# Three weight blocks of a folded product: turned by DMA in place of TensorE

## The chip, the cores and the metric

The kernel runs on one core of one Trainium2 chip. The metric is the device time of one execution in microseconds; the time before is the median of three runs. A profile shows one further execution, instruction by instruction. TensorE (PE) multiplies matrices, VectorE (DVE) and ScalarE (ACT) work on elements, GpSimd (POOL) does little here, and SyncE (SP) issues most DMAs.

## The reference

Attention without softmax is computed for 8 batches of 8 heads (576 tokens, 64 columns each), normalised, and fed as x (4608 x 512) to a multiplicative network:

```python
kv = np.einsum('bhsd,bhse->bhde', k, v)
out = np.einsum('bhsd,bhde->bhse', q, kv)
rms = np.sqrt(np.mean(out * out, axis=-1, keepdims=True) + 1e-06)
x = (out / rms * g_norm)        # then (B,H,S,D) -> (B*S, H*D)
a = x @ w1                      # 512 x 1024
b = x @ w2                      # 512 x 1024
h = a * b @ w3                  # 1024 x 1024
out = h @ w_out                 # 1024 x 512
```

The weights arrive as 64-bit floats, and the kernel makes 32-bit floats of them by itself.

## The kernel before, in words

There is no nonlinearity between w3 and w_out. The kernel therefore starts with a **fold**: it computes the product w3 @ w_out (1024 x 512) once and keeps it in `w3o_sb`. All the rest, for groups of 512 tokens, works with `w1`, `w2` and that product, by a fast matrix multiplication with seven products (lines L727, L1019, L1277).

The fold has two halves: half 0 takes the upper 512 rows of w3, half 1 the lower 512. Each half runs over eight chunks `c` of 128 columns of w3 and 128 rows of w_out (`KF` = 8). For a chunk, `fold_chunk` (L696) adds four products of 128x512 into four PSUM banks, one for each 128 rows `m`. TensorE needs its left operand transposed, so `turn_w3` (L683) first turns the four 128x128 blocks of a chunk by TensorE into a PSUM bank, and ScalarE copies that bank (L688) to the chunk's place in the tile `ab`. There are four such places, so chunks 4 and 5 write where chunks 0 and 1 stood. The profile records each 128x512 product as two matmul rows, and a chunk's four transposes as four.

Data come in this way. `load_next` issues on SP's queue the next load of a raw 64-bit tile `raw` (four buffers; a tile comes as a pair of DMAs). The conversion of a tile is ScalarE's L161 and L163, then VectorE's L165, L169, L172 and L175 (and L135 where a scale is applied). `begin_next` writes ScalarE's part, `end_next` writes VectorE's part and then the next load. For half 1 a raw tile holds two chunks of w3: chunks 2 and 3 are converted in step c = 0 of the second loop, chunks 4 and 5 in step c = 2, chunks 6 and 7 in step c = 4. Tiles of w1 and w2 are converted in the steps between.

Into the eight steps of half 1 the attention of batch 0 is woven: `begin_q` transposes q by TensorE (L358, copied by ScalarE, L360), `begin_kv` computes kv (L338, copied by L346 and L348), `product` multiplies them (L416). Its normalisation is ScalarE's L383 (squares), VectorE's L384, ScalarE's L388 (root), VectorE's L390 and L393, which write `xn`. Then `x_first` turns half of `xn` by DMA: ScalarE splits it into low and high 16-bit words (L297), SP issues two 16-bit DMA transposes (L301), and ScalarE joins the words (L311). The other half is transposed by TensorE (L452). These transposes and products, and those of chunks, share three PSUM banks (`ps_at`) in rotation; the sums of the fold lie in others.

What sets the order: in this part of the program all engines' instructions stand in the order in which the program writes them (`tc.manual_schedule` over the engines). An engine takes its own instructions strictly in that order and waits on semaphores for the others; SP's queue of DMA issues is such an order too. Behind the fold the order of VectorE and ScalarE is set by a scheduler.

Of the kernel before, what the change touches and what calls it, by code (L numbers as in the profile page):

```python
# [22 lines left out]
def kernel(  # L23
# [32 lines left out]
    nc = tc.nc  # L56
    PSUM = bass.MemoryType.PSUM
    P = 128
# [5 lines left out]
    KF = DF // P  # L64
# [19 lines left out]
    def bank(pool, tag):  # L84
        return pool.tile([P, 512], FP32, name=tag, tag=tag)
# [6 lines left out]
    def load_q(b, r):  # L92
        t = loaded["q", b, r] = inp.tile([P, 2, J * D], FP32, name="q_sb")
        nc.sync.dma_start(
            out=t, in_=q[b, 2 * r:2 * r + 2, 0:G, :].rearrange("h (p j) d -> p h (j d)", j=J)
        )
# [20 lines left out]
    ab = [ab_all[:, i] for i in range(2)]  # L117
# [71 lines left out]
    raws = []  # L189

    def raw_tile():
        return conv_pool.tile([P, 1024], w1.dtype, name="raw", bufs=RAW)

    def load_next():
        if len(raws) == len(todo):
            return
        what, i = todo[len(raws)]
        raw = raw_tile()

        def load(where, src):  # L200
            nc.sync.dma_start(out=raw[:, where].rearrange("p (c m) -> p c m", c=src.shape[1]), in_=src)

        if what == "w":
            for n, w in enumerate((w1, w2)):
                src = w[:, i * P:(i + 1) * P].rearrange("(c p) f -> p c f", p=P)
                load(slice(n * 512, (n + 1) * 512), src)
        elif what == "b":
            for h in range(2):
                src = w3[DF // 2:DF, (2 * i + h) * P:(2 * i + h + 1) * P]
                load(slice(h * 512, (h + 1) * 512), src.rearrange("(m p) f -> p m f", p=P))  # L210
        else:
            src = w3[0:DF // 2, i * P:(i + 1) * P].rearrange("(m p) f -> p m f", p=P)
            cols = w_out[i * P:(i + 1) * P, :].rearrange("p (c f) -> p c f", c=1)

            n = 1 if i else 2
            for h in range(n):
                load(slice(h * 512 // n, (h + 1) * 512 // n), src[:, h * NH // n:(h + 1) * NH // n, :])
            for h in range(n):
                f = slice(h * DM // n, (h + 1) * DM // n)
                load(slice(512 + f.start, 512 + f.stop), cols[:, :, f])  # L220
        raws.append(raw)
# [28 lines left out]
    def end_next(load=True):  # L250
        for c in begun[len(converted)]:
            all_of(c)
        converted.append(len(converted))
        if load:
            load_next()

    def all_of(steps):
        for _ in steps:
            pass
# [14 lines left out]
    def keep_warm(n):  # L274

        t = bank(ps_mm, "mm")
        for _ in range(n):
            nc.tensor.matmul(t[:, 0:P], lhsT=ident, rhs=ident, start=True, stop=True)

    def turn_by_dma(srcs, apart, turned, dsts, copy=nc.gpsimd.tensor_copy):  # L280

        def words(t):
            return t.bitcast(U16).rearrange("p ... (n w) -> p ... n w", w=2)

        def planes(t, i, n):
            t = t.bitcast(U16).rearrange("p (w n) -> p w n", w=2)
            size = 4 * P // n  # L290
            return t[:, :, i * size:(i + 1) * size]

        for i, src in enumerate(srcs):
            to = planes(apart, i, len(srcs))
            if len(src.shape) == 3:
                src, to = words(src), to.rearrange("p w (a n) -> p w a n", a=src.shape[1])
                copy(to, src.rearrange("p a n w -> p w a n"))  # L297
            else:
                copy(to, words(src).rearrange("p n w -> p w n"))
        yield  # L300
        nc.sync.dma_start_transpose(  # L301
            out=turned.bitcast(U16).rearrange("p (a t) -> p a t", t=P), in_=apart.bitcast(U16)
        )
        yield
        for i, dst in enumerate(dsts):
            src = planes(turned, i, len(dsts))
            if len(dst.shape) == 3:
                src = src.rearrange("p w (a n) -> p a n w", a=dst.shape[1])
            else:
                src = src.rearrange("p w n -> p n w")  # L310
            copy(words(dst), src)  # L311
# [364 lines left out]

    w3T = {}

    def turn_w3(half, c):
        t_ps = bank(ps_at, "at").rearrange("p (m f) -> p m f", m=NH)  # L680
        for m in range(NH):
            src = chunks[:, c, 0, m * P:(m + 1) * P]
            nc.tensor.transpose(t_ps[:, m, :], src, ident)  # L683

        w3T[half, c] = ab[c % 4 // 2][:, c % 2].rearrange(
            "p i (a f) -> p (i a) f", f=P
        )
        nc.scalar.copy(w3T[half, c], t_ps)  # L688

    sums_ps = {}  # L690

# [701 lines left out]
    chunks = fold.tile([P, KF, 2, DM], FP32, name="chunks")  # L1393
    with tc.manual_schedule(
        engines={mybir.EngineType.DVE, mybir.EngineType.Activation, mybir.EngineType.SP}
    ):
        for _ in range(RAW):
            load_next()
        nc.scalar.activation(const.tile([P, 1], FP32, name="warm"), eps_col, AF.Sqrt)
        g_row = const.tile([1, P], FP32, name="g_row")  # L1400
        for e in range(2):
            nc.scalar.dma_start(
                out=g_row[:, e * D:(e + 1) * D], in_=g_norm.rearrange("(o d) -> o d", o=1)
            )


        keep_warm(14)
        begin_next()
        end_next()
        turn_w3(0, 0)  # L1410
        keep_warm(6)
        begin_next()

        g_ps = bank(ps_at, "at")[:, 0:1]
        nc.tensor.transpose(g_ps, g_row, ident[0:1, 0:1])
        nc.scalar.copy(g_col, g_ps)
        for c in range(KF):

            if c > 2:
                begin_next()  # L1420
            end_next()
            if c == 4:
                load_four("k", 0, 0)
                load_q(0, 0)
            elif c == 5:
                load_four("v", 0, 0)
                load_q(0, 1)
                load_q_left(0)
            if c == 0:
                for n in range(2):  # L1430
                    fold_chunk(0, c, range(NH), slice(n * N, (n + 1) * N))
                begin_next(lambda: turn_w3(0, 1))
                keep_warm(2)
                continue
            fold_chunk(0, c, range(NH - 1))
            if c < 3:
                begin_next(lambda: turn_w3(0, c + 1), 2)
            else:
                turn_w3(*((0, c + 1) if c + 1 < KF else (1, 0)))
            fold_chunk(0, c, [NH - 1])  # L1440


        first = batch(0)
        first.start()
        BEGIN, PRODUCT = {1: 0, 4: 1}, {2: 0, 5: 1}
        norms = {}
        FIRST = len(converted) + KF - 1
        for c in range(KF):
            if c in BEGIN:
                first.begin_q(2 * BEGIN[c], 2 * BEGIN[c] + 1)  # L1450
                if c == max(BEGIN):
                    x_first = first.x_by_dma(0, nc.scalar.copy)
                    next(x_first)
                    next(x_first)
            if c - 1 in norms:
                all_of(norms[c - 1])
            if c < KF - 2:
                if c < max(BEGIN):
                    begin_next()
                if c == max(BEGIN) + 1:  # L1460
                    all_of(x_first)

                end_next(len(raws) < FIRST)
            elif c == KF - 2:
                run(sum_w(0))
            fold_chunk(1, c, [0])
            if c in BEGIN:
                first.begin_kv(BEGIN[c])
                if c == max(BEGIN):
                    load_q_left(1)  # L1470
            if c + 1 == KF:
                for r in range(2):
                    first.turn(2 + r)
                run(combine_x(0))
                end_next(False)
                for _ in range(3):
                    load_next()
            fold_chunk(1, c, range(1, NH - 1))
            if c + 1 < KF:
                turn_w3(1, c + 1)  # L1480
            if c in (max(BEGIN), KF - 2):
                begin_next()
            fold_chunk(1, c, [NH - 1])
            if c in PRODUCT:
                norms[c] = first.product(PRODUCT[c])
                next(norms[c])
                next(norms[c])
    fold_cm.__exit__(None, None, None)
    late_pool = ctx.enter_context(tc.tile_pool(name="late", bufs=1, reuse_waits="tile"))
# [6 lines left out]
    for n, T in enumerate(groups):  # L1496
# [29 lines left out]
        if T in IN_TWO:  # L1526
            p = 2
# [130 lines left out]
```

## Time and profile before

| | before |
|---|---|
| median of 3 runs | 742.34 us (741.92 to 742.8) |
| the profiled execution's own time | 742.22 us |
| its span, first to last instruction | 740.4 us |
| TensorE busy | 734.6 us |
| VectorE busy | 623.3 us |
| ScalarE busy | 379.4 us |
| mean granted TensorE clock | 1.000 |
| half 1 of the fold on TensorE | about 42 to 81 us |

Times in the profile are microseconds from the start of the span. A row of the order of time has the start, the length, the engine, the line of the program and the operation, the tiles (written <- read), and in brackets the engine's idle time ahead of it with what ended it. Such a length includes the time in which an instruction drains while the next begins, so the distance from one start to the next is what an instruction costs. A DMA has the time of its issue and, apart from it, the time from issue to landing.

### The profile page before, as it was taken

What the parts mean: (1) busy time and instruction counts of PE and PEld (TensorE: products, weight loads), DVE (VectorE), ACT (ScalarE), POOL (GpSimd) and SP (SyncE); (2) the same over time, 40 slices, a digit from 0 to 9 for tenths busy, and PEclk for the clock granted to TensorE, in tenths of its full rate; (3) what the DMA queues carried; (4) which work ended last, traced back from release to release, by engine and by line L of the source; (5) the groups of instructions that cost most, each with busy time, mean ns of one, the idle gap of its engine ahead of it and who ended that gap; (6) DMA issues with size and microseconds to landing.
All of it is one profiled execution on the core that took longest, in us unless ns stands there. A gap on an engine that the chain in (4) does not pass through costs nothing.

```text
span 740.4 us, 16858 instructions
## 1 busy us (share of the span) xinstructions
PE 734.6 (99%) x6845; PEld 659.8 (89%) x6845; DVE 623.3 (84%) x1253; ACT 379.4 (51%) x662; POOL 21.6 (3%) x29
## 2 busy tenths in 40 slices
PE   8999999999999999999999999999999999999998
PEld 6455788888899999999999999999999999999997
DVE  7967898967869689968996899689969987997797
ACT  6787777515552675257526752576177313212321
POOL 0000000131000000000000001000001000000000
PEclk9999999999999999999999999999999999999999
DMA  9997834599999698869886988688846762565454
GB/s 312 338 357 228 237 108 137 136 333 305 314 267 323 175 279 261 267 166 293 251 266 161 302 251 266 175 288 234 269 103 220 227 207 87 184 214 158 135 199 136
DMA packets 135457, 169.66 MB, mean 229 GB/s; under 512 B 78036, under 2 KB 110804, under 8 KB 135380
## 3 DMA queue, kind: packets, MB, share of 16 engines
q1 hardware_dynamic: 132928, 154.16, 69.1%
q10 hardware_dynamic: 2452, 14.42, 5.7%
q8 instruction: 54, 0.88, 0.5%
q14 instruction: 23, 0.19, 0.1%
HBM read 130.55 MB, written 20.71 MB: 204 GB/s over the span
## 4 chain that ended last, share of the span: by engine, by line
PE 98%; DVE 1%; DMA 1%; issue 0%; SPq 0%; ACT 0%
PE mm L727 38%; PE mm L1277 23%; PE mm L1019 21%; PE mm L696 7%; PE at L338 3%; PE at L727 2%; PE mm L416 1%; PE at L416 1%; PE at L683 1%; DMA raw<-in_moe_w_out_dram 1%; PE at L1320 0%; PE at L435 0%; PE at L358 0%; DVE ab L165 0%; DVE chunks L172 0%
## 5 line engine op out<-in xcount | busy, mean ns | idle before, releaser
L1068 ACT COPY slots<-mm 128x512 f32<-128x512 f32 x88 | 51.6, 586 | 126.2 <-PE mm L1277 83.1
L727 PE MATMUL mm<-xT,w_sb 128*128 128x256 f32 x448 | 102.9, 379 | 0.0
L727 PEld LDWEIGHTS mm<-xT,w_sb 128*128 128x128 f32 x448 | 84.5, 190 | 11.3 <-issue 0.5
L727 PE MATMUL mm<-xc,ws 128*128 128x256 f32 x336 | 76.1, 379 | 0.0
L727 PEld LDWEIGHTS mm<-xc,ws 128*128 128x128 f32 x336 | 64.0, 190 | 8.6
L745 ACT COPY slots<-mm 128x512 f32<-128x512 f32 x59 | 34.7, 587 | 69.5 <-PE mm L727 64.5
L696 PE MATMUL mm<-chunks,ab 128*128 128x512 f32 (+1 forms) x136 | 60.4, 579 | 0.4 <-DVE chunks L175 0.3
L1072 DVE TENSOR_TENSOR slots<-mm,slots 128x512 f32<-128x512 f32 x66 | 45.2, 684 | 17.4 <-PE mm L1019 17.3
L1069 ACT COPY slots<-mm 128x384 f32<-128x384 f32 x88 | 42.3, 481 | 25.8 <-PE mm L1277 23.0
L1019 PE MATMUL mm<-ws,w3o_sb 128*128 128x128 f32 x350 | 54.0, 275 | 0.0
L384 DVE TENSOR_REDUCE inv<-sq 128x8 f32<-128x512 f32 (+1 forms) x40 | 24.6, 630 | 31.6 <-ACT sq L383 31.6
L1277 PE MATMUL mm<-w3o_sb,ab 128*128 128x128 f32 x368 | 48.9, 276 | 0.0
L1019 PEld LDWEIGHTS mm<-ws,w3o_sb 128*128 128x128 f32 x350 | 46.4, 192 | 0.0
L1277 PEld LDWEIGHTS mm<-w3o_sb,ab 128*128 128x128 f32 x368 | 45.4, 192 | 0.6
L1277 PE MATMUL mm<-w3o_sb,raw 128*128 128x128 f32 x340 | 43.5, 275 | 0.0
L696 PEld LDWEIGHTS mm<-chunks,ab 128*128 128x128 f32 x136 | 23.2, 190 | 21.4 <-issue 13.4
L1277 PEld LDWEIGHTS mm<-w3o_sb,raw 128*128 128x128 f32 x340 | 40.7, 192 | 0.0
L727 PE MATMUL mm<-xc,w_sb 128*128 128x256 f32 x160 | 38.5, 384 | 0.0
L727 PE MATMUL mm<-xT,ws 128*128 128x256 f32 x160 | 38.1, 381 | 0.0
L1073 DVE TENSOR_TENSOR slots<-mm,slots 128x384 f32<-128x384 f32 x66 | 36.4, 552 | 1.9 <-PE mm L1277 1.9
L311 ACT COPY xT<-xn 128x1024 uint16<-128x1024 uint16 x28 | 32.5, 1168 | 3.1 <-DMA xn<-xT 3.1
L727 PEld LDWEIGHTS mm<-xT,ws 128*128 128x128 f32 x160 | 30.1, 190 | 4.2 <-ACT slots L745 0.2
(243 smaller groups left out, 1643.9 us busy)
## 6 DMA issues: line engine op xcount, KB each, us to landing
w3o_sb<-w_l SPq DMA_DIRECT2D x21, 896.0 KB, 5.0
w3o_sb<-w3o_l SPq DMA_DIRECT2D x18, 896.0 KB, 6.6
raw<-in_moe_w_dram SPq DMA_DIRECT2D x31, 512.0 KB, 8.0
raw<-w3o_l SPq DMA_DIRECT2D x15, 896.0 KB, 4.7
w3o_sb<-w3o_l ACTq DMA_DIRECT2D x14, 896.0 KB, 4.5
k_sb<-in_k_dram SPq DMA_DIRECT2D x16, 576.0 KB, 4.9
v_sb<-in_v_dram SPq DMA_DIRECT2D x16, 576.0 KB, 6.1
q_sb<-in_q_dram SPq DMA_DIRECT2D x32, 256.0 KB, 4.5
```

The lines of the kernel that those rows point to most:

```text
L311: copy(words(dst), src)
L338: nc.tensor.matmul(ps[r * D:(r + 1) * D, :], lhsT=k_sb[rows, r, cols], rhs=v_sb[rows, r, cols], start=(j == 0), stop=(j == JS - 1),)
L384: adds["norm"] = nc.vector.tensor_reduce(out=inv[:, i], in_=sq.rearrange("p (h d) -> p h d", d=D), axis=AX.X, op=ALU.add)
L696: nc.tensor.matmul(sums_ps[half][m][:, cols], lhsT=w3T[half, c][:, m, :], rhs=chunks[:, c, 1, cols], start=(c == 0 and cols.start == 0), s ...
L727: nc.tensor.matmul(ps[:, u, :], lhsT=lhsT(a_name, u, c), rhs=rhs(b_name, c),  start=(u == 0 and c == 0 and new), stop=(c == chunks - 1), s ...
L745: copies.setdefault(name, []).append(nc.scalar.copy(t, ps))
L1019: nc.tensor.matmul(ps[place // 4][:, place % 4, :], lhsT=x, rhs=y, start=new and place // 4 not in seen, stop=True, skip_group_check=True,)
L1068: nc.scalar.copy(z[:, 0:4], ps[0])
L1069: return nc.scalar.copy(z[:, 4:7], ps[1][:, 0:3])
L1072: nc.vector.tensor_add(z[:, 0:4], ps[0], z[:, 0:4])
L1073: nc.vector.tensor_add(z[:, 4:7], ps[1][:, 0:3], z[:, 4:7])
L1277: nc.tensor.matmul(ps[place // 4][:, place % 4, :], lhsT=x[:, c, :], rhs=y[:, c, :], start=new and place // 4 not in seen, stop=(c == 1), ...
```

## The change

Chunks 3, 4 and 5 of half 1 are no longer turned by TensorE. `w3_by_dma` reads the chunk as 16-bit words: VectorE copies its low and high words apart into the chunk's place in `ab` (L299), SP's queue issues one 16-bit DMA transpose of 128x1024 from there back onto the natural chunk (L301), and ScalarE joins the words into the place in `ab` (L311), where TensorE finds the transposed chunk.

The split and the transpose of chunk 3 stand in step c = 0 behind the conversion of chunks 2 and 3, those of chunks 4 and 5 in step c = 2 behind theirs. In both steps the next load is now issued behind the transposes. The joins stand in ScalarE's order as follows: chunk 3 behind the conversion's L161/L163 of step c = 2; chunk 4 between L383 and L388 of the first normalisation; chunk 5 behind the two L297 of `x_first`. Chunks 0 to 2, 6 and 7 are turned as before. Behind the fold, every engine's instructions stand in the same order as before.

```diff
-    def turn_by_dma(srcs, apart, turned, dsts, copy=nc.gpsimd.tensor_copy):
+    def turn_by_dma(srcs, apart, turned, dsts, copy=nc.gpsimd.tensor_copy, split=None):
...
-                copy(to, words(src).rearrange("p n w -> p w n"))
+                (split or copy)(to, words(src).rearrange("p n w -> p w n"))
...
+    def place_w3(half, c):
+        w3T[half, c] = ab[c % 4 // 2][:, c % 2].rearrange("p i (a f) -> p (i a) f", f=P)
+        return w3T[half, c]
...
+    def w3_by_dma(c):
+        natural, to = chunks[:, c, 0, :], place_w3(1, c).rearrange("p m f -> p (m f)")
+        return turn_by_dma(
+            [natural], to, natural, [to], nc.scalar.copy, split=nc.vector.tensor_copy
         )
...
+        turns, SPLIT = {}, {0: (3,), 2: (4, 5)}
         for c in range(KF):
             if c in BEGIN:
                 first.begin_q(2 * BEGIN[c], 2 * BEGIN[c] + 1)
                 if c == max(BEGIN):
                     x_first = first.x_by_dma(0, nc.scalar.copy)
                     next(x_first)
                     next(x_first)
+                    all_of(turns[c + 1])
...
-                end_next(len(raws) < FIRST)
+                end_next(False)
+                for i in SPLIT.get(c, ()):
+                    turns[i] = w3_by_dma(i)
+                    next(turns[i])
+                    next(turns[i])
+                if len(raws) < FIRST:
+                    load_next()
...
-            if c + 1 < KF:
+            if c == 2:
+                all_of(turns[c + 1])
+            elif c + 1 < KF and c + 1 not in turns:
                 turn_w3(1, c + 1)
...
                 norms[c] = first.product(PRODUCT[c])
                 next(norms[c])
+                if c == 2:
+                    all_of(turns[4])
                 next(norms[c])
```

More of the change, by code (lines that the diff above doesn't have):

```diff
@@ L296, in turn_by_dma @@
                 src, to = words(src), to.rearrange("p w (a n) -> p w a n", a=src.shape[1])
-                copy(to, src.rearrange("p a n w -> p w a n"))
+                (split or copy)(to, src.rearrange("p a n w -> p w a n"))
             else:
-                copy(to, words(src).rearrange("p n w -> p w n"))
+                (split or copy)(to, words(src).rearrange("p n w -> p w n"))
         yield
@@ L683, in turn_w3 @@
             nc.tensor.transpose(t_ps[:, m, :], src, ident)
-        w3T[half, c] = ab[c % 4 // 2][:, c % 2].rearrange(
-            "p i (a f) -> p (i a) f", f=P
+        nc.scalar.copy(place_w3(half, c), t_ps)
+    def w3_by_dma(c):
+        natural, to = chunks[:, c, 0, :], place_w3(1, c).rearrange("p m f -> p (m f)")
+        return turn_by_dma(
+            [natural], to, natural, [to], nc.scalar.copy, split=nc.vector.tensor_copy
         )
-        nc.scalar.copy(w3T[half, c], t_ps)
     sums_ps = {}
```

## The prediction

> **What bounds the kernel now.** I read four views of the profile in this order: busy times and the chain that ended last, the chain piece by piece in the fold, ScalarE's order of time there, and the DMA share.
>
> Page, busy times and chain:
>
> ```profile
> PE 734.6 (99%) x6845; PEld 659.8 (89%) x6845; DVE 623.3 (84%) x1253; ACT 379.4 (51%) x662; POOL 21.6 (3%) x29
> ...
> PE 98%; DVE 1%; DMA 1%; issue 0%; SPq 0%; ACT 0%
> ```
>
> TensorE is busy for 734.6 of 740.4 us and is 98% of the chain, so an instruction removed from it is time saved, as long as nothing else becomes late. The product lines behind the fold (L727, L1019, L1277) show 0.0 us of idle time, so a microsecond won or lost in the fold stays to the end. Chain in order of time, the second half of the fold:
>
> ```profile
> 54.79 0.44 PE at L683 x4
> ...
> 59.95 0.44 PE at L683 x4
> ...
> 66.35 0.44 PE at L683 x4
> ```
>
> These are the transposes of chunks 3, 4 and 5 (counted from 0): 0.44 us each.
>
> ScalarE, order of time (start, length, what; in brackets the idle time before it):
>
> ```profile
> 57.23 1.09 ACT L383 ACTIVATE sq<-at 128x512 f32<-128x512 f32 x2 [1.38 <-PE at L416]
> 59.17 0.31 ACT L388 ACTIVATE inv<-inv,eps_col 128x16 f32<-128x16 f32 x1 [0.86 <-DVE inv L384]
> 59.38 1.13 ACT L161 ACTIVATE ab<-raw 128x1024 f32<-128x1024 uint32 x1
> ...
> 62.91 1.99 ACT L297 COPY xT<-xn 128x1024 uint16<-128x1024 uint16 x2
> ...
> 66.82 0.59 ACT L688 COPY ab<-at 128x512 f32<-128x512 f32 x1 [0.71 <-PE at L683]
> ...
> 71.53 0.60 ACT L688 COPY ab<-at 128x512 f32<-128x512 f32 x1
> ```
>
> From 59.17 to 72.13 ScalarE has only that one hole of 0.71 us. The last row is the copy of chunk 6's transposes; TensorE begins chunk 6 (L696) at 72.62, only 0.5 us behind it. So ScalarE is the second limit in just this stretch. DMA by stretches (DMA share and GB/s are the last two columns):
>
> ```profile
> 52.00:56.00 4.00, 4.00 (x13) 1.77 (x12) 0.47 (x1) 2.54 (x3) 0.00 (x0) 1.00 1.06 382
> 56.00:60.00 4.00, 4.00 (x73) 2.44 (x73) 1.67 (x4) 1.92 (x4) 0.00 (x0) 1.00 1.02 363
> 60.00:64.00 4.00, 4.00 (x72) 2.49 (x74) 3.93 (x6) 4.00 (x7) 0.00 (x0) 1.00 0.35 91
> ```
>
> The 16 DMA engines are full until about 60 us. This is what the new transposes meet.
>
> **The change, part by part.**
>
> *Removed.* On TensorE 3 x 4 transposes, 3 x 0.44 = 1.31 us on the path that sets the end. On ScalarE three L688 copies, about 0.48 us each from start to start (61.49 to 61.96).
>
> *Added on VectorE.* Three splits of 128x1024 uint16. VectorE's nearest row is L165, same shape and type, 0.76 us; ScalarE's L297 (1.05 us) bounds it from above, L901's 0.42 us from below. I take 0.76. The first falls into the idle stretch 42.68 to 43.63, before L165; at 1.05 it pushes L165 by 0.1 us. The other two follow the conversion of chunks 4 and 5, which ends at 52.46, where VectorE idles 5.39 us (until L384 at 57.86). They cost nothing at either bound, and are done by 54.0 (54.6).
>
> *Added on SP's queue.* Three transposes, each 1.24 to 1.3 us of issue (rows L301). The first stands ahead of the load pair of the last w3 chunks (issued 41.82 and 42.69 before): it waits for the split, is issued at 43.5, and the pair moves to about 45 to 46. Its ScalarE user starts at 59.38, and the trace's loads land at most 9.8 us after issue: covered. The q loads behind (46.45) and the w and k, v loads keep their issue times. The second and third stand behind k and v (49.0, 50.0) and ahead of the w pair of 50.71, which moves to about 56 and is needed at 76.42: covered. No DMA comes free of its queue earlier.
>
> *When they land.* The trace has loads landing in the order of issue, a pair's second 1.4 to 1.5 us behind its first. v, issued at 50.00, lands 8.9 us later, at 58.9. What does a transpose do in such a queue? Row L301 issued at 81.55 lands 4.1 us later, at 85.65; the load before it (issued 74.94, 9.7 us) lands at 84.6. So: about 1.0 us behind its forerunner, not the 2.7 us from issue of a free queue. Four queued near 206 us land at 214.5, 215.4, 216.2, 217.2, 0.9 us apart. Then:
> - chunk 3: forerunner lands at 48.36 (39.95 + 8.4), it at 49.4. ScalarE reaches its join (after L163, which ends at 53.96) much later; join done at 55.0; TensorE wants it at 57.11 - 0.44 = 56.7. Hidden.
> - chunk 4: v is delayed by chunk 3's passage, 58.9 + 1.0 = 59.9; the transpose lands at T = 60.9. Bounds: free queue, 53.4 + 2.8 = 56.2; a passage of 1.4 us each (the spacing of the two transposes at 64.93 and 66.35, set by their issue), 61.7. I take 60.9, from the row with the same situation.
> - chunk 5: T + 0.9.
>
> *Added waits on ScalarE.* The order of the changed program puts the join of chunk 4 (L311) between the two L383 and L388. L383 end at 58.32 - 0.44 = 57.9, so ScalarE stands still from 57.9 to T, 3.0 us. Behind it are queued L388, without which VectorE can't normalise (L390, L393) and free the PSUM banks that L358 and L338 need, then the conversion L161/L163, and all copies up to chunk 6. From T the queue runs without a hole, by the spacing of the rows: join 1.06 (L311, 69.41 to 71.53 for two), L388 0.21, L161 and L163 2.11, two L360 0.95, two L297 1.89, join of chunk 5 1.06, kv copies 1.31, L161 and L163 2.10, two L311 2.12, L688 of chunk 6 0.60. Sum 13.41. TensorE's chunk 6, which began at 72.62, begins at T + 13.4.
>
> **The sum.** Break-even is T = 72.62 - 13.41 = 59.2. With T = 60.9 TensorE is 1.7 us late there, having spent its 1.31 us and more in waits at L358 (bank, freed by L393 at about T + 2.4 = 63.3) and L696. VectorE's chain ends up about 0.3 us later still, L390 being late: but L452, which needs it, starts 0.9 us behind L393 now. After that, nothing recovers. The profiled execution took 742.22 us with a span of 740.4, 0.12 us under the median of the runs shown (742.34); the 1.8 us around the span stay: 742.22 + 1.7 = **743.9 us**.
>
> [...] The row says 0.9 to 1.0 us per transpose in the queue. [...]
>
> **Rivals.**
> 1. *The transposes are in time* (faster). If T is at or below 57.9, the join fills the 0.86 us hole before L388 and its 1.06 us shifts L388 by little. Chunk 6 then follows its copy at 57.9 + 13.4 = 71.3, that is 1.3 us earlier: 740.9; with the 0.25 us that TensorE now loses around 62.1 (L358 to L338 takes 2.08 us from 61.08, 1.83 us from 45.81) at most 740.7. It decides at T = 59.2. For it: issue is possible at 53.4, 4.5 us ahead, and a free queue needs 2.8. Against it: v itself lands at 58.9 already now.
> 2. *In between*: the queue moves faster without the w pair beside it, T from 58 to 60: 741.0 to 743.0. For it: some DMA engines run ahead (the w pair's data are all in by about 60). [...]
> 3. *More is late*: xn's two transposes, after L297 at T + 6.2, have 4.4 us until ScalarE's L311, and need 4.2 (64.93 to 69.1). If these slip, or the loads of 69.58 to 77.6, moved by some 2 us, miss their conversions, add 1 us or more: 744.7 to 746.
> 4. *It does nothing that counts*: the removed transposes were cover for waits that stay. 742.2; contained in 2.
>
> **How the numbers follow.** Forecast case (T from 60.0 to 61.7: 743.0 to 744.7) 0.58; rival 1 0.15; rivals 2 and 4 0.17; rival 3 0.10. The range 740.9 to 744.9 leaves out part of rivals 1 and 3 only. About 0.2% (1.5 us) can be told from no change by a measurement of this kernel: the forecast lies just at the bound, 743.8. Slower by more: most of the forecast case above 743.8, and rival 3: 0.5. Faster by more (below 740.86): the better part of rival 1: 0.1. Within: 0.4.
>
> **What would show it.** In the changed profile: ScalarE idle about 3 us before the second L311 on ab, released by the DMA on chunks; L388 at about 62 instead of 59.17; TensorE waiting at L358 or L338 for VectorE's xn and at L696 for ScalarE's ab; chunk 6's L696 group at 74.3 instead of 72.6. I am wrong if chunk 4's transpose lands before 59 (the queue is not in order, or the share of v is done earlier), or if L338 and L696 show no new waits; then 741 is right.

## The result, and the profile after

| | before | changed |
|---|---|---|
| median of 6 runs each | 742.37 us (741.92 to 742.80) | 747.46 us (744.93 to 748.26) |
| ratio, 95% interval | | 1.0062 [1.0051, 1.0073] |
| the profiled execution's own time | 742.22 us | 748.05 us |
| its span | 740.4 us | 746.3 us |
| mean granted TensorE clock | 1.000 | 0.998 |

The change makes the kernel 5.1 us slower: 3.6 us above the forecast of 743.9, and 2.6 us above the upper end of the range. The line numbers of the changed kernel are higher: L683 is now L687, L688 is L689, L696 is L703, L727 is L734, L1277 is L1284.

Page after, chain that ended last, by engine:

```profile
PE 94%; DVE 2%; DMA 2%; ACT 1%; issue 1%; SPq 0%; POOL 0%; ACTq 0%; DVEq 0%; POOLq 0%
```

TensorE's share of the chain was 98%. The 4% that left it belong to DMA, VectorE, ScalarE and "issue". The same chain in order of time (start, length, what) says where:

```profile
52.65 0.72 DVE ab L299 x2
53.37 8.89 DMA chunks<-ab
62.29 0.04 issue
62.33 0.07 ACT ab L311
...
64.88 1.06 PE at L358 x4
```

For 8.89 us the end of the program hangs on one DMA: chunk 4's transpose, from its issue at 53.37 to its landing. ScalarE after, order of time (in brackets the idle time ahead of the row and what ended it):

```profile
54.12 1.14 ACT L311 COPY ab<-chunks 128x1024 uint16<-128x1024 uint16 x1
56.98 1.09 ACT L383 ACTIVATE sq<-at 128x512 f32<-128x512 f32 x2 [1.72 <-PE at L416]
62.33 1.16 ACT L311 COPY ab<-chunks 128x1024 uint16<-128x1024 uint16 x1 [4.27 <-DMA chunks<-ab]
63.39 0.30 ACT L388 ACTIVATE inv<-inv,eps_col 128x16 f32<-128x16 f32 x1
...
75.18 0.59 ACT L689 COPY ab<-at 128x512 f32<-128x512 f32 x1
```

Chunk 3's join shows no wait, chunk 4's shows 4.27 us, and L388, at 59.17 before, begins at 63.39. The copy of chunk 6 ends at 75.77, that is 13.44 us behind the join's start. TensorE after:

```profile
60.40 0.60 PE L358 MATMUL at<-ident,q_sb 128*128 128x128 f32 x4
64.88 1.06 PE L358 MATMUL at<-ident,q_sb 128*128 128x128 f32 x4 [3.89 <-ACT ab L161]
65.74 1.91 PE L703 MATMUL mm<-chunks,ab 128*128 128x512 f32 x2
67.58 1.60 PE L338 MATMUL at<-v_sb,k_sb 64*64 64x64 f32 x72
...
76.84 2.84 PE L703 MATMUL mm<-chunks,ab 128*128 128x512 f32 x6
```

TensorE stands still for 3.89 us. The releaser is put down to ScalarE's L161, at 63.60 and done at 64.7, while VectorE's xn (L390 at 63.73 after 4.84 us of idle time, L393 at 64.09) frees the same bank; both stand behind the join. Behind the standstill the rows are longer than their like: L703 x2 takes 1.91 us, 1.02 us elsewhere. Chunk 6 begins at 76.84, 4.22 us later than before (72.62), though ScalarE's copy was done 1.07 us ahead of it. The reason is in the stretches (third column from the end: granted clock):

```profile
62.00:64.00 2.00, 0.00 (x0) 0.00 (x0) 0.25 (x1) 1.67 (x3) 0.00 (x0) 1.00 0.94 210
64.00:66.00 2.00, 1.12 (x5) 1.15 (x6) 1.91 (x4) 2.00 (x3) 0.00 (x0) 0.73 1.06 372
66.00:68.00 2.00, 2.00 (x18) 0.49 (x21) 1.93 (x4) 2.00 (x4) 0.00 (x0) 0.50 0.77 261
```

From about 64.9 to 68.3 us TensorE is granted half its clock.

### The profile page after: what moved, and what is told of

It reads as the page before. It is cut to its first block, busy times and chain, and to the rows that moved or that the text cites. A ratio compares the mean times of both kernels' runs of the same rounds, so it can differ in the third digit from the quotient of the medians.

```text
span 746.3 us, 16846 instructions
## 1 busy us (share of the span) xinstructions
PE 736.7 (99%) x6833; PEld 660.3 (88%) x6833; DVE 625.5 (84%) x1256; ACT 380.9 (51%) x662; POOL 21.9 (3%) x29
## 4 chain that ended last, share of the span: by engine, by line
PE 94%; DVE 2%; DMA 2%; ACT 1%; issue 1%; SPq 0%; POOL 0%; ACTq 0%; DVEq 0%; POOLq 0%
PE mm L734 36%; PE mm L1284 23%; PE mm L1026 21%; PE mm L703 6%; PE at L338 2%; PE at L734 2%; DMA chunks<-ab 1%; PE mm L278 1%; PE mm L416 1%; PE at L416 1%; PE at L687 1%; PE at L1327 0%; ACT ab L161 0%; DMA out_dram<-raw 0%; PE at L435 0%
## 5 line engine op out<-in xcount | busy, mean ns | idle before, releaser
L734 PE MATMUL mm<-xT,w_sb 128*128 128x256 f32 x448 | 102.9, 379 | 0.0
L734 PEld LDWEIGHTS mm<-xT,w_sb 128*128 128x128 f32 x448 | 84.4, 190 | 11.5 <-issue 0.5
L734 PE MATMUL mm<-xc,ws 128*128 128x256 f32 x336 | 76.1, 379 | 0.0
L734 PEld LDWEIGHTS mm<-xc,ws 128*128 128x128 f32 x336 | 63.8, 190 | 8.7
L703 PE MATMUL mm<-chunks,ab 128*128 128x512 f32 (+1 forms) x136 | 60.7, 584 | 0.3 <-ACT ab L689 0.2
L1284 PE MATMUL mm<-w3o_sb,ab 128*128 128x128 f32 x368 | 48.9, 276 | 0.0
L1284 PEld LDWEIGHTS mm<-w3o_sb,ab 128*128 128x128 f32 x368 | 45.4, 192 | 0.7
L703 PEld LDWEIGHTS mm<-chunks,ab 128*128 128x128 f32 x136 | 23.8, 192 | 22.4 <-issue 15.3
L1284 PE MATMUL mm<-w3o_sb,raw 128*128 128x128 f32 x340 | 43.5, 275 | 0.0
L1284 PEld LDWEIGHTS mm<-w3o_sb,raw 128*128 128x128 f32 x340 | 40.7, 192 | 0.0
L734 PE MATMUL mm<-xc,w_sb 128*128 128x256 f32 x160 | 38.6, 384 | 0.0
L734 PE MATMUL mm<-xT,ws 128*128 128x256 f32 x160 | 38.2, 382 | 0.2 <-ACT slots L752 0.2
L311 ACT COPY xT<-xn 128x1024 uint16<-128x1024 uint16 x28 | 32.5, 1169 | 5.4 <-DMA xn<-xT 5.4
L734 PEld LDWEIGHTS mm<-xT,ws 128*128 128x128 f32 x160 | 30.0, 190 | 4.8 <-ACT slots L752 0.7
```

The lines of the kernel that those rows point to most:

```text
L703: nc.tensor.matmul(sums_ps[half][m][:, cols], lhsT=w3T[half, c][:, m, :], rhs=chunks[:, c, 1, cols], start=(c == 0 and cols.start == 0), s ...
L734: nc.tensor.matmul(ps[:, u, :], lhsT=lhsT(a_name, u, c), rhs=rhs(b_name, c),  start=(u == 0 and c == 0 and new), stop=(c == chunks - 1), s ...
L1284: nc.tensor.matmul(ps[place // 4][:, place % 4, :], lhsT=x[:, c, :], rhs=y[:, c, :], start=new and place // 4 not in seen, stop=(c == 1), ...
```

## The experiments

**Theory A:** the loss is the late landing of whatever transpose stands behind full loads, with ScalarE's queue and TensorE behind it. **Theory B**, the rival: the added transposes cost by their traffic, wherever they stand. C (code position) and D (how a transpose passes a full queue) came up on the way. "Shift" is by how much TensorE is later than before at a place. The count of runs of the kernel before that an experiment is compared with lies between 9 and 28; their medians lie between 742.17 and 742.49 us.

### e1_chunk3: only chunk 3 by DMA

```diff
-        turns, SPLIT = {}, {0: (3,), 2: (4, 5)}
+        turns, SPLIT = {}, {0: (3,)}
```

(The joins of chunks 4 and 5 go with it.)

> Only chunk 3 is turned by DMA; chunks 4 and 5 by TensorE as before. Theory A (the loss is the wait for chunk 4's late transpose): no new wait on ScalarE or TensorE, 0.44 us of TensorE saved, 741.8 to 742.0 us. Theory B (the added 16-bit transposes and their traffic slow the rest, wherever they stand): a third of the loss stays, about 744 us. The load behind chunk 3's transpose tells what one passage through a full queue costs: 1.0 us by the prediction, 1.8 us if the changed kernel's landings (k: 57.45 before, 59.82 after, of which 0.6 was there ahead of the transpose) are read so.

741.93 us, ratio 0.9994 [0.9986, 1.0003]. The join (54.16) shows no wait, and no new wait stands anywhere. The transpose with a late user cost nothing here, though it passed the same queue. Theory B's 744 us are out.

### e2_w_behind and e3_kv_w_behind: loads moved behind the transposes of chunks 4 and 5

```diff
-                if len(raws) < FIRST:
-                    load_next()
+                for _ in range({1: 0, 2: 2}.get(c, 1)):
+                    if len(raws) < FIRST:
+                        load_next()
```

e3 moves the k and v loads of step c = 1 as well.

> As the changed kernel, but one pair of w1/w2 loads (1 MB) is issued behind the transposes of chunks 4 and 5 instead of ahead of them. Theory A: chunk 4's transpose lands about 2.9 us earlier, near 59.5 instead of 62.2; TensorE's delay at the end of the fold falls by as much, from 4.2 us to 0.3 to 1.3 us; 742.5 to 743.5 us. Theory B: the traffic is the same, so still about 747 us.

> As the run before, and the k and v loads of the second half of the heads also go behind the transposes. Theory A: chunk 4's transpose meets a nearly empty queue and lands at 56 to 57.9, ahead of ScalarE's join; no wait stays, 1.3 us saved: 740.7 to 741.2 us, unless k and v, now landing near 60 to 61, come too late for their use at about 62. Theory B: about 747 us.

e2: 745.50 us, 1.0043 [1.0030, 1.0056]; e3: 748.00 us, 1.0084 [1.0069, 1.0100]. In e2 chunk 4 is joined at 58.96 after a wait of 1.56 us, in e3 at 57.94 with none. So the landing answers to what is ahead of it in the queue. Both times are missed all the same (742.5 to 743.5 and 740.7 to 741.2 were expected), because the next transposes now stand behind the moved loads: in e2 xn's joins wait 1.56 us and TensorE 2.15 us at chunk 6. ScalarE in e3:

```profile
57.94 1.16 ACT L311 COPY ab<-chunks 128x1024 uint16<-128x1024 uint16 x1
...
72.64 2.21 ACT L311 COPY xT<-xn 128x1024 uint16<-128x1024 uint16 x2 [3.97 <-DMA xn<-xT]
```

TensorE's chunk 6 in e3:

```profile
75.51 4.29 PE L705 MATMUL mm<-chunks,ab 128*128 128x512 f32 x6 [4.14 <-ACT ab L691]
```

The wait has only changed its place: 4.27 us at chunk 4 became 3.97 us at xn, with 3.4 us of half clock behind it as well (4.29 us for the six rows, 2.84 in the changed kernel). That is the mechanism of the prediction's rival 3, in a kernel where its condition holds.

### e4_warm: TensorE kept busy through the standstill

```diff
             for r in rs:
+                if b == 0 and r == 3:
+                    keep_warm(14)
                 q_t(r)
```

> As the changed kernel, with 14 idle products (128x128, results unused) on TensorE between the two q transposes where it stands still for 3.9 us. Theory A with its second part (the halved clock from 64.9 to 68.3 is due to that standstill and costs about 1 us): the clock stays at 1.00 there, the delay at the end of the fold falls from 4.2 to about 3.2 us, 745.5 to 746.5 us. If the clock has nothing to do with the standstill or costs nothing: unchanged, 747 to 748 us.

746.61 us, 1.0058 [1.0045, 1.0071]. In the profiled execution (745.66 us) the join is as late as ever, 62.73, but the clock stays at 1.000, and chunk 6 begins 3.64 us late in place of 4.22, with 0.4 us more of lateness in the join. By the prediction's sum 62.73 means 62.73 - 59.2 = 3.5 us. So the standstill is worth its own length, and the half clock about 1 us on top. The shift of 3.64 then stays the same to the end. The cover isn't sure: two of the four executions still have a mean clock of 0.998, and they took 747.14 and 747.98 us, the two at 1.000 took 745.66 and 746.09.

### e5_reordered and e6_reordered_pad: all loads behind the next transposes

Order on SP's queue: transposes of chunks 4 and 5, k, v, w pair, xn's two transposes, q loads, w pair.

```diff
-                if len(raws) < FIRST:
+                if c == 2:
+                    load_four("kv", 0, 1)
+                if c not in (1, 3) and len(raws) < FIRST:
                     load_next()
...
-                first.begin_kv(BEGIN[c])
+                first.begin_kv(BEGIN[c], load=c != 1)
...
-                first.begin_q(2 * BEGIN[c], 2 * BEGIN[c] + 1)
+                first.begin_q(2 * BEGIN[c], 2 * BEGIN[c] + 1, load=c == 1)
...
                     next(x_first)
+                    for r in (2, 3):
+                        first.load_q_ahead(r)
```

e6 adds four idle products: `keep_warm` 14, 6 and 2 become 16, 7 and 3.

> All three chunks stay turned by DMA. On SP's queue the k and v loads and the w pair of step c = 2 stand behind the transposes of chunks 4 and 5, and the q loads and the w pair of step c = 4 behind xn's two transposes, so that no load stands ahead of a transpose with an early user. Theory A (the loss is the late landing of whatever transpose stands behind full loads): chunk 4 lands at about 56.7 and its join shows no wait, xn's transposes land by about 68 to 69 and L311 on xT shows at most a few tenths, TensorE is 0.9 to 1.3 us earlier than before at 80 us; 740.9 to 741.4 us, with 0.9 us more if the stall near 487 us is there. Theory B (the transposes cost by the traffic itself, wherever they stand): TensorE still 1 us or more late at 80 us and 744 or more.

> As e5, with four more idle 128x128 products on TensorE at the start, which shift every later instruction of TensorE's program by four (eight with the weight loads). Theory C (the 'issue' wait of 0.7 to 1.0 us at L416 near 487 us depends on where this code lies in the program): e5 and e6 differ in this wait, in one of them it is absent and that one is 0.7 to 1.0 us faster, less at most 0.3 us for the idle products. Rival (it depends on the data traffic of the moment, or on chance): the same wait in both or in neither, e6 0 to 0.3 us slower.

e5: 743.75 us, 1.0023 [1.0014, 1.0032]; e6: 742.77 us, 1.0008 [0.9999, 1.0016]. Neither theory's number. The fold does what A says. TensorE in e5:

```profile
71.30 2.84 PE L705 MATMUL mm<-chunks,ab 128*128 128x512 f32 x6 [0.21 <-ACT ab L691]
```

Chunk 6 begins 1.32 us earlier than before, with all three chunks turned by DMA. But the loads that gave way are late further on. ScalarE in e5:

```profile
83.12 1.13 ACT L161 ACTIVATE ab<-raw 128x1024 f32<-128x1024 uint32 x1 [1.94 <-DMA raw<-in_moe_w_dram]
```

This takes 1.65 us back (the shift goes from -1.32 to +0.33 at 85 us). About 0.4 us more is lost near 488 us in the middle of L416, in e5 and not in e6.

### e7_chunks35 and e10_35_q_behind: chunk 4 back on TensorE

```diff
-        turns, SPLIT = {}, {0: (3,), 2: (4, 5)}
+        turns, SPLIT = {}, {0: (3,), 2: (5,)}
```

The join of chunk 4 goes with it. e10 also issues the q loads of step c = 4 behind xn's transposes, as in e5.

> Chunk 4 is turned by TensorE again, chunks 3 and 5 by DMA, the loads in the order of the changed kernel. Theory A: chunk 5's transpose lands at about 61 to 62.5, and its join stands behind the two L297 on xn (64.3), so nothing waits for it; xn's transposes land behind it and the w loads, at about 69 to 70. TensorE saves 8 of 12 transposes, 0.87 us: 741.4 us, up to 742.3 if L311 on xT waits some tenths. Theory B (traffic): 743 or more.

> Chunks 3 and 5 by DMA, chunk 4 by TensorE, and the two q loads of step c = 4 issued behind xn's two transposes in place of ahead of them. Theory A: xn's transposes land at 66.7 and 68.0, the wait of 0.92 us at L311 on xT and the one of 0.97 at chunk 6 go, TensorE is 1.3 us earlier than before from 66 us on; the six w loads start about 1 us later and land by 80, ahead of their users at 81. 741.0 us (740.7 to 741.4). Rival: the loads behind become late instead (ScalarE waits for a raw tile near 76 or 81): 741.7 or more.

e7: 741.75 us, 0.9993 [0.9984, 1.0002]; e10: 741.33 us, 0.9987 [0.9978, 0.9996]. Chunk 5's join stands 6 us later on ScalarE than chunk 4's, and shows no wait in either. What remains in e7 is xn's landing:

```profile
69.38 2.23 ACT L311 COPY xT<-xn 128x1024 uint16<-128x1024 uint16 x2 [0.92 <-DMA xn<-xT]
```

and in e10 0.29 us of it:

```profile
69.22 2.24 ACT L311 COPY xT<-xn 128x1024 uint16<-128x1024 uint16 x2 [0.29 <-DMA xn<-xT]
```

e10 is faster than before by 0.13%, inside its forecast (740.7 to 741.4). xn's transposes still stand behind a w pair there, and TensorE waits 0.36 us at chunk 6.

### e8_join_later: chunk 4's join moved behind L388, L161 and L163

```diff
                 if c < max(BEGIN):
                     begin_next()
+                if c == 3:
+                    all_of(turns[4])
...
-                if c == 2:
-                    all_of(turns[4])
```

> The changed kernel with chunk 4's join moved on ScalarE behind L388 and the conversion's L161 and L163. The landing stays at about 62.3. Theory A (the cost is the work of ScalarE queued behind the wait): L388 is on time at 59.2, no wait of VectorE or of L358 on it; ScalarE waits about 0.8 us before the join, from 61.5 to 62.3, and 11.1 us of work follow, so chunk 6 begins at 73.4 to 73.8 in place of 76.8 and TensorE keeps its full clock: 743.0 to 743.8 us. Rival (the landing itself binds TensorE through chunk 4's own product, whoever waits): TensorE waits 2 us or more before chunk 4's L696, 745 or more.

745.17 us, 1.0035 [1.0023, 1.0048]. ScalarE in e8:

```profile
58.79 0.31 ACT L388 ACTIVATE inv<-inv,eps_col 128x16 f32<-128x16 f32 x1 [0.86 <-DVE inv L384]
...
61.38 1.16 ACT L311 COPY ab<-chunks 128x1024 uint16<-128x1024 uint16 x1 [0.17 <-DMA chunks<-ab]
```

In the fold A holds: the wait of 4.27 us is 0.17, TensorE waits 1.29 us at chunk 4's product, and chunk 6 begins at 73.45 (expected 73.4 to 73.8). The time is above the forecast all the same. The span grew by 3.4 us: TensorE is 0.83 us late behind the fold, loses 2.0 us more between 180 and 266 us, in small waits, and 0.77 us near 490 us. The changed kernel has such losses too: 0.84 us and 0.98 us.

### e9_plain_copy: chunk 3's transpose replaced by an ordinary copy

```diff
+        if plain:
+            nc.sync.dma_start(out=turned.bitcast(U16), in_=apart.bitcast(U16))
+        else:
             nc.sync.dma_start_transpose(
```

`plain` is set for chunk 3 alone; this kernel leaves chunk 3 unturned.

> The changed kernel with one DMA replaced: chunk 3's 16-bit transpose becomes an ordinary copy of the same 262 KB between the same two tiles, at the same place of SP's queue (so chunk 3 is left unturned; all else is as it was). Theory D (a transpose in full queues makes the engines that are ahead stand still until the slowest has come to it, and so costs about 1.8 us where its bytes cost 0.7): k and v land about 1 us earlier than in the changed kernel (k near 58.6 in place of 59.8), no gap in the packets near 48 us, and chunk 4 lands at about 61.2; 746 us. Rival (it is the added bytes, written and read, whatever the kind of DMA): k lands at 59.5 to 60, chunk 4 at 62 and more, the time that of the changed kernel, 747 to 748.

746.37 us, 1.0053 [1.0040, 1.0067]. From the landing of the w3 load ahead of chunk 3's DMA to the landing of k it takes 9.09 us before, 10.88 in the changed kernel, 10.90 to 10.95 in e1, e4, e7, e8 and e12 (10.74 in e10), and 9.27 in e9. So the transpose delays the queue by 1.65 to 1.86 us, a copy of the same bytes by 0.18. (The 0.7 us of theory D is an estimate: 262 KB at the 363 GB/s of the stretch 56 to 60 us before are 0.72 us.) Stretches of the changed kernel (last two columns: DMA share, GB/s):

```profile
46.50:47.00 0.50, 0.50 (x6) 0.50 (x5) 0.50 (x1) 0.36 (x1) 0.00 (x0) 1.00 1.14 326
47.00:47.50 0.50, 0.50 (x3) 0.07 (x1) 0.50 (x1) 0.50 (x2) 0.00 (x0) 1.00 3.13 226
47.50:48.00 0.50, 0.50 (x10) 0.17 (x13) 0.46 (x2) 0.50 (x2) 0.00 (x0) 1.00 0.68 93
48.00:48.50 0.50, 0.50 (x44) 0.50 (x44) 0.35 (x1) 0.50 (x1) 0.00 (x0) 1.00 0.29 37
48.50:49.00 0.50, 0.50 (x44) 0.47 (x33) 0.17 (x1) 0.50 (x2) 0.00 (x0) 1.00 0.87 197
```

and one of the same stretches in e9:

```profile
48.00:48.50 0.50, 0.50 (x45) 0.50 (x43) 0.32 (x1) 0.50 (x1) 0.00 (x0) 1.00 1.11 360
```

The 16 engines move 350 to 360 GB/s throughout in e9. At the transpose they fall to 37 with loads still queued: the five stretches move 879 / 5 = 176 GB/s on the mean in place of 350, so 1.25 us worth of full rate is missing. The engines aren't idle by the profile: the share of 3.13 in the second stretch belongs to packets that begin there and end long after it. The single packets in the trace's DMA records say why. Chunk 3's transpose is made of 1024 packets of 256 bytes, most of which take 0.018 us. But 19 of them begin one after another from 47.11 to 48.36 us and all end at 48.66 to 48.70, just behind the last 1024-byte packet of the loads ahead, which begins at 48.27. So what is ahead stands in a transposing packet until the slowest has come to it, as theory D says; in e9 the DMA share of the same stretches stays at 1.07 to 1.11. That the packets which stand belong to different engines is inferred. Of e9's expectation, k near 58.6 is met (58.5), and chunk 4's landing near 61.2 too (join at 61.04).

### e11_all_in_time: e6, and batch 1's loads behind the last w pairs

```diff
                 for _ in range(3):
                     load_next()
+                load_four("kv", 1, 0)
+                load_q_left(1)
```

> e6 (all three chunks by DMA, loads behind the transposes, four idle products more at the start) with the k, v and q-left loads of batch 1, whose users come at 120 us and later, issued behind the last three w pairs in place of ahead of them. Theory A: the w pair of 82 us lands 2 us earlier than in e6, near 80.5, and the waits of 1.6 us on ScalarE's L161 and on L727's bank near 85 us go; TensorE stays 1.3 us earlier than before: 741.0 to 741.4 us. Rival (the DMA queues are simply full from 68 us on, and what is moved up makes another load late): 742 or more.

741.60 us, 0.9990 [0.9981, 0.9999], 0.2 us above its forecast. The waits near 83 and 85 us are gone, as A says. xn's landing still costs 0.36 us, and v's 0.29 at L338.

### e12_changed_pad: the changed kernel with four idle products more

```diff
-        keep_warm(14)
+        keep_warm(16)
...
-        keep_warm(6)
+        keep_warm(7)
...
-                keep_warm(2)
+                keep_warm(3)
```

> The changed kernel with only the four idle products of e6 more at TensorE's start. Theory C (the 'issue' wait at L416 near 490 us goes with the place of the code in TensorE's program, not with the lateness of the fold): the wait of 0.70 us is absent, TensorE is still some 4.2 us later than before at 80 us with the clock at 0.5 for 3.41 us, and the time is about 0.9 us below the changed kernel's: 746.3 to 746.9. If the small losses between 180 and 232 us (0.75 us in the changed kernel) are of the same kind they go too: 745.6 to 746.0. Rival (both come from the late fold and the DMA traffic behind it): both stay, 747.5 or a little more.

746.32 us (743.69 to 748.08), 1.0063 [1.0049, 1.0077]. The row of the changed kernel

```profile
493.58 0.21 PE L416 MATMUL at<-kv_sb,qT 64*64 64x64 f32 x1 [0.70 <-issue]
```

has no counterpart here: no idle time shows at L416. C is right on that. But the rest of its expectation was wrong for the profiled execution: the loads ahead of the transposes were issued some 1.5 us earlier this time, so the join came at 60.51, the standstill was 2.45 us, and the clock stayed at 1.000. TensorE in e12:

```profile
63.06 0.63 PE L358 MATMUL at<-ident,q_sb 128*128 128x128 f32 x4 [2.45 <-ACT ab L161]
...
73.98 2.84 PE L703 MATMUL mm<-chunks,ab 128*128 128x512 f32 x6 [0.47 <-ACT ab L689]
```

This execution took 743.69 us. The other four have a mean clock of 0.995 to 0.997 and took 745.95 to 748.08. So the pad's effect on the median can't be read from this run; its effect on the wait can.

## Why the prediction was right in direction and wrong in size

The steps that failed are terms of the sum: chunk 3's passage through the queue was put at 1.0 us and took 1.8, and the half clock after a standstill (1.1 us) and the losses behind the fold (1.8 us) were put at nothing.

- **TensorE's 1.31 us, VectorE's splits: right.** The splits took 0.65 to 0.70 us in idle stretches. With nothing in the way (e5), TensorE gained 1.32 us by chunk 6, and began it at 71.30, the time that the prediction's rival 1 gave (71.3).
- **SP's issue times: wrong, without harm at the users.** The three transposes took 2.48, 4.42 and 3.21 us to issue, where 1.24 to 1.3 was forecast. k, said to keep its time, was issued at 50.34 in place of 49.01; the pair behind chunk 3's transpose at 46.3 (45 to 46 forecast), and the w pair at 61.2 (56 forecast). No conversion of these tiles waited.
- **The wait, its place and the queue behind it: right.** Join between L383 and L388, L388 late, L358 starved, sum of 13.41 us: measured 13.44 (75.77 - 62.33), and in e12 60.51 to 73.98, 13.47 us. The wait forecast at L696 shows where the clock stays whole (0.47 us in e12). There, T - 59.2 is the answer to within 0.2 us: e12's T = 60.51 gives 742.22 + 1.3 = 743.5, measured 743.69; e4's 62.73 gives 745.7, measured 745.66.
- **T itself: wrong by 1.4 us** (60.9 forecast, 62.33 measured). The term that failed is chunk 3's passage through the queue, put at 1.0 us from rows where transposes follow each other or a queue that runs dry. By what it delayed behind it (k, e9) it is 1.8 in a full queue, 0.8 us more. Another 0.6 us is the w3 load ahead, which landed at 48.94 in place of 48.36. The second passage, v to chunk 4, was as forecast in the changed kernel (k to join 2.51 us, forecast 1.45 + 1.0); in e4 it was 3.9 us, and why is open. T lies between 60.5 and 62.7 in the profiled executions with this load order, and the upper bound of 61.7 was too low.
- **The clock: missing.** A standstill was priced at its own length, and nothing was put for what follows it. Half clock over 3.4 us made chunk 6 begin 1.07 us behind its copy. Of the changed kernel's six executions, five have a mean clock of 0.995 to 0.998 and took 746.41 to 748.26; the sixth, at 1.000, took 744.93.
- **"After that, nothing recovers": true, and too little.** 0.84 us were lost between 180 and 266 us, and 0.98 us near 490 us, of which 0.70 us is the "issue" wait. The sum had no term for either.
- **The sum again** for the profiled execution, growth of the span: 1.7 forecast + 1.4 (T) + 1.1 (clock) + 0.84 + 0.98 = 6.0 us; measured 746.3 - 740.4 = 5.9.
- **The rivals.** Rival 1's condition, T at or below 57.9, is met by the load orders of e3, e5 and e11, not by the changed one; its time of 740.9 is reached by none of them, since each is late at a later place. Rival 2's range of T is that of e2 (58.96). Rival 3 did not happen in the changed kernel (L311 on xT at 72.91 without a wait), but does in e2 and e3. Rival 4 is out: e5 gains the 1.32 us in the fold.
- **DMA or TensorE, chunk by chunk.** In this load order chunk 4, whose result is wanted 9 us after its split, was better left to TensorE (e7, 741.75 us, where the changed kernel takes 747.46), and chunks 3 and 5 were not (e10, 741.33 us). Chunk 4 too is turned by DMA without loss in the load order of e11 (741.60 us). In the queue full of loads a transpose cost 1.8 us against 0.18 for a copy of the same bytes (e9).

Open: the losses between 180 and 266 us. They show as several small waits (0.41 us at a load of w3o_sb in e8, 0.18 us at ScalarE's slots in the changed kernel), in the changed kernel, e2, e3, e8 and e9, hardly in e4 (3.64 us late) or e12 (0.23 us), and in e11 with 0.43 us though TensorE is early there. So lateness alone does not explain them. Which of the queues starts them was not tried.

## What to carry to other kernels

Ahead of a DMA transpose, count the loads that stand before it in the queue and give it their landing plus 1 us or more (here 1.1 us, and 2.4 in e4, taking v 1.45 us behind k). Add to the loads that stand behind it what its passage cost here, 1.65 to 1.86 us in a full queue. Then look at what is queued behind the instruction that will wait for it: the same transposes met no wait in chunks 3 and 5 and made TensorE 3 us late in chunk 4 (62.33 - 59.2), where chunk 3's own passage is part of the lateness. Moving loads behind the transpose helps only if the next transpose, and the next user of those loads, are looked at in the same way; it took three such steps (e3, e5, e11) until no large wait was left. And a new wait on TensorE of the length of e9's (2.62 us) or more is to be priced with the clock that it may lose, about 1 us here.

## What the runs showed of the hardware

- **A transpose held up a full DMA queue.** It cost what stood behind it 1.65 to 1.86 us for 262 KB, where an ordinary copy cost 0.18 (e9), with the DMA rate down to 37 GB/s in half a microsecond, while 19 packets stood for up to 1.57 us and ended together (changed kernel).
- **TensorE's clock.** Profiled standstills of 3.89 us (changed), 4.14 (e3) and 2.62 (e9) were followed by a clock of 0.5 for 3.4 us; those of 2.45 (e12) and 2.15 us (e2) were not. The trace's clock records have the half clock of the changed kernel from 64.92 to 68.33 us, 3.413 us long, and the stretches of full clock around it 58.03 and 679.25 us long, 17 and 199 times as much; in the kernel before, one stretch of full clock lasts 737.28 us, 216 times. In the 3.413 us just ahead of the fall, TensorE stood still for 3.38 us in the changed kernel, 3.41 in e3 and 2.21 in e9. Why 2.62 us in e9 was followed by the half clock and 2.45 us in e12 was not is open.
- **The place of code.** The "issue" wait inside L416 near 490 us (0.43 to 0.70 us) is there in the changed kernel, e2, e3, e8 and e9, and as a loss of about 0.4 us in e5. All have TensorE programs of the same length, twelve products shorter than before. No such wait shows before and in e1, e4, e6, e7, e10, e11 and e12, whose programs have other lengths (e10 loses 0.15 us at the same place). Four idle products at the start remove it, with the fold early (e6) or late (e12). The trace's DMA records fit the fetching of instructions as the cause. In the changed kernel a 16384-byte packet of the instruction queue q8 begins at 491.38 us, 0.58 us behind the start of the run of small products (L338, then L416) at 490.80, and the late row starts 2.20 us after the packet, at 493.58; before, the packet begins at 483.20, 2.52 us ahead of the run. In all six kernels such a packet begins as the run begins, from 0.12 us ahead of it to 0.58 us behind, and the late row starts 2.17 to 2.41 us after that packet. In e10, with 0.15 us lost, the packet is 0.48 us ahead of the run, and in the other seven 0.72 to 5.29 us ahead. The step from this timing to the cause is inferred.
